# Four input and three output buffers, rows of four tokens, earlier token lists and an earlier first fetch in a causal mixing and expert kernel

## The chip, the cores and the metric

The kernel runs on one core of one Trainium2 chip. The core's engines run side by side, each through its own list of instructions in order: TensorE (PE, with its weight loads as PEld), VectorE (DVE), ScalarE (ACT), GpSimd (POOL) and SyncE (SP). An instruction that must wait for another engine or for a transfer holds everything behind it on its own engine. Transfers (DMA) are issued from SP, ACT and POOL and carried out by 16 DMA engines that all three share. The metric is device time in microseconds, the median of several runs.

## The reference, cut to what matters

```python
def _attn_ref(x, weight):                      # x (8, 3584, 192), weight (8, 7)
    w = softmax(weight, axis=-1)
    x_pad = np.concatenate([zeros((B, 6, D)), x], axis=1)
    x_unf = x_pad[:, idx, :].reshape(B, S, 7, 8, 24)      # the token and the six before it
    return einsum('hk,bskhg->bshg', w, x_unf).reshape(B, S, D)

def _moe_ref(x, w_gate, w1, w2):               # x (28672, 192); 8 experts, F = 1024
    cap = N // E                               # 3584 tokens for each expert
    logits = x @ w_gate
    order = np.argsort(-logits.flatten())      # the best pairs of token and expert first
    ...                                        # a pair is taken if its token is free and its expert has room
    for e in range(E):
        mask = assigned == e
        out[mask] = np.maximum(x[mask] @ w1[e], 0.0) @ w2[e]
```

Each of 8 heads mixes a token with the six tokens before it by 7 softmax weights. Each of the 28672 mixed tokens then goes through exactly one of 8 experts, and each expert takes exactly 3584 tokens, chosen greedily by logit.

## The kernel before

**Convolution.** The tokens are cut into 16 half batches of 1792. `load(i)` brings a half batch from DRAM to a tile `X`, 118 partitions (112 tokens and the six before them) by 16 windows by 192, in two transfers on SP: a small one for the six rows, a large one for the 112. There are three such buffers. `conv(i)` multiplies the tile, head by head, with a banded matrix `TH` on TensorE (`cv`), and ACT copies each head from PSUM to a tile `a`, of which there are two. After the eighth head ACT issues the transfer of `a` to the DRAM tensor `attn`, one row of 192 floats (768 bytes) per token, in the order of the tokens.

**Logits.** VectorE transposes `a` in 32 x 32 blocks into `aT` (`transp`, four instructions per half batch); TensorE multiplies by the gate weights (`logits`, products `pl`), ACT copies to `L`, TensorE transposes `L` (`pt`, in `logits_t`), VectorE adds a mask `pm` into the table `LT` and takes the maximum over the experts (`top`). Inside `conv(i)` the function `mid(h)`, called after each head's product, issues the transposes of half batch i - 1 with heads 0 to 3 and the logits of i - 2 with heads 2 and 5; `end(i - 2)` follows after head 7.

**Routing.** Everything from logits to lists of tokens is a row of generators: `half(0)` (threshold, placement, sorting and lists of the first eight half batches), `tail` and `tail2` (logits of half batches 14 and 15), `half(1)`, `rest`, `last`. `Steps.hook` puts their instructions between others: a planner (`Pace`) keeps an estimate of the time at which each engine will have come so far, and a step is issued when VectorE and ACT are not too far ahead of TensorE by that estimate. `tokens` turns a list's sorted entries into token numbers `ia0`, `ia`, `ib0`, `ib`.

**Feed-forward.** 56 tiles of 512 tokens. POOL fetches a tile's rows from `attn` by token number (`gather`, four indirect transfers); rows of short lists are cleared beforehand. TensorE transposes them (`px`), ACT and VectorE split them into a high and a low part (`evac`: `xa`, `xd`). `l1` makes eight blocks `ph` of hidden units, which ACT (`hh`) and VectorE (`hl`) split; `l2` makes `y` from them; `store` scatters `yo` to `out` by token number. The weights are loaded by SP into four buffers `raw`, split by ACT (high) and POOL or VectorE (low) in `wsplit`, and written to DRAM for later use; each split frees a buffer for SP's next load. The pools of the tiles (`wpool`, `wpool2`, `fh0` and others) take over the space of the convolution's buffers.

The first two tiles come from the first half of the tokens: `first(0)` and `first(1)` gather them as soon as `half(0)` has been issued. With the planner's pace that is in the last half batch; the transposes and splits of tile 0 stand behind all of the convolution.

Of the kernel before, what the change touches and what calls it, by code (L numbers as in the profile page):

```python
# [5 lines left out]
F32 = mybir.dt.float32  # L6
# [10 lines left out]
G = 256  # L17
# [95 lines left out]
def build(ctx, tc, nc, x, weight, wg, attn, LT, wk):  # L113
# [48 lines left out]
    pm = wk.tile([128, 16], F32, name="pm")  # L162

    def gate_ops():
# [9 lines left out]
        V.tensor_scalar(pi, pi, 16, None, op0=OP.bitwise_and)  # L174
        V.memset(pm, 0.0)
        for b in range(4):
            V.tensor_scalar(pm[:, 4 * b + 3:4 * b + 4], pi, -1.0 / 16, None, op0=OP.mult)
# [4 lines left out]
    def load(i):  # L182
        t = X[i] = k.xp[i % 3].tile([118, 16, D], F32, name="X")
# [10 lines left out]
    def conv(i, mid):  # L194
# [8 lines left out]
        A.dma_start(attn[i * 1792:(i + 1) * 1792].rearrange("(w p) d -> p w d", p=W), a[0:W])  # L203
# [10 lines left out]
    def transp_last(u):  # L214

        i = NHB - 1
        a = wk.tile([128, 16, 64], F32, name="X%d" % u)
        for q in range(2):
            V.transpose(a[:, 8 * q:8 * q + 8], AA[i][:, 8 * q:8 * q + 8, 64 * u:64 * u + 64])
        AT[i] = AT[i] + [a] if u else [a]  # L220

    def logits(i, u):

        if u == 0:
            AT[i].append(k.bank("pl"))
        pl = AT[i][-1]
        for c in range(4):
            w = slice(4 * c, 4 * c + 4)
            t = AT[i][u // 2].rearrange("p w (c t) -> p w c t", t=32)[:, w, u % 2] if i == NHB - 1 else AT[i][0][:, w, u]
            PE.matmul(pl[32 * c:32 * c + 32, 0:128], GF[:, u], t, start=(u == 0), stop=(u == 5))  # L230
# [13 lines left out]
    k.toeplitz, k.gate_ops, k.transp_last = toeplitz, gate_ops, transp_last  # L244
# [18 lines left out]
class Route:  # L263

# [268 lines left out]
    def tokens(self, nt, idx, e1=8, t1=None):  # L533
# [10 lines left out]
        i = v(wk.tile([128, 128], I32, name="m_j"))  # L544
        off = wk.tile([128, 1], F32, name="off")
# [16 lines left out]
    def lists(self, F, nt, h, base, idx, *part):  # L562
# [6 lines left out]
        yield from self.tokens(nt, idx, *part)  # L569
# [240 lines left out]
class General:  # L810


    def __init__(self, ctx, tc, ltab, attn, w1, w2, out, ident, drm):
# [4 lines left out]
        self.list = drm.tile([NTOK, 1], I32, name="glist")  # L818

    def consts(self):  # L820
# [20 lines left out]
        self.idi = p.tile([128, G], I32, name="g_idi")  # L841
        V.tensor_copy(self.idi, self.id)
# [131 lines left out]
    def lists(self):  # L974
# [25 lines left out]
        i1 = p.tile([128, 1], I32, name="g_i1")  # L1000
        with tc.For_i(0, G, 1) as g:
            V.tensor_copy(s1, si[:, bass.ds(g, 1)])
            V.tensor_copy(i1, self.idi[:, bass.ds(g, 1)])
# [4 lines left out]
    def ffn(self):  # L1008
# [5 lines left out]
        ix = p.tile([128, 1], I32, name="g_ix")  # L1014
# [7 lines left out]
        with tc.For_i(0, NE, 1) as e:  # L1022
# [3 lines left out]
            with tc.For_i(0, CAP // 128, 1) as t:  # L1026
                nc.sync.dma_start(ix, self.list[bass.ds(e * CAP + t * 128, 128)])
                P.indirect_dma_start(out=x, out_offset=None, in_=self.attn,
                                     in_offset=bass.IndirectOffsetOnAxis(ap=ix, axis=0),
# [15 lines left out]
                P.indirect_dma_start(out=self.out, out_offset=bass.IndirectOffsetOnAxis(ap=ix, axis=0),  # L1045
# [8 lines left out]
class FFN:  # L1054
# [19 lines left out]
    def wpool(self, ctx, j):  # L1074
        self.wpa[j] = ctx.enter_context(self.tc.tile_pool(name="wpa%d" % j, bufs=1))
# [214 lines left out]
    def run(self, idx_of, at, eng, free):  # L1290
# [4 lines left out]
        for i in range(n + 1):  # L1295
            at(i)
            if i + 2 < n:
                self.gather(i + 2, idx_of(tiles[i + 2]))
# [18 lines left out]

NL = 3


def moe_kernel(ctx, tc, x, weight, wg, w1, w2, out):
# [6 lines left out]
    with ExitStack() as cw:  # L1328
# [16 lines left out]

        order = [(e, (0,)) for e in range(NE)]
# [10 lines left out]
        def half(h):  # L1357
# [6 lines left out]
            yield from r.lists(r.F, TA, h, 0 if h else None, *((ia,) if h else (ia0, 8, 4)))  # L1364
# [190 lines left out]
```

## Time and profile before

| | us |
|---|---|
| median of three runs | 1328.89 |
| the runs | 1336.24, 1327.68, 1328.89 |
| the profiled execution's own time | 1324.88 |
| its span, first to last instruction | 1323.1 |

Busy in the span: TensorE 1251.3 us (95%), its weight loads 1077.4, VectorE 1005.2, ACT 543.2, POOL 540.1. The mean granted clock of TensorE is 0.973. The transfers moved 188.29 MB; the queue of ACT (q10, the writes of `attn`) carried 22.02 MB in 28928 pieces.

How to read the lines below. In a row of the stretches each engine's busy time in that stretch is followed by its number of instructions; then come TensorE's granted clock, the DMA engines' busy share, and GB/s. In the timeline a row has the start, the duration, the engine (a q behind it: the engine's issue of a transfer), the line of the kernel, the operation, the tile written and the tiles read, and in brackets how long the engine stood idle before and what ended that. In the chain a row is a piece of the sequence that ended last: start, length, and the work, or the transfer, it consisted of. A row of the waits names who waited, for whom, how long in total, how often, and the longest.

### The profile page before, as it was taken

The page shows a single profiled execution, that of the slowest core. Times are in us where ns is not written, and L with a number is a line of the kernel's source. Part 1 is how long each engine was busy: PE and PEld are TensorE (multiplying, and loading weights), DVE is VectorE, ACT ScalarE, POOL GpSimd, SP SyncE. Part 2 cuts the span into 40 slices and gives each one's busy share as a digit, 9 for nine tenths or more (in the row PEclk, how much of TensorE's full clock was granted, in tenths as well). Part 3 has the DMA queues.
Part 4 walks back from the last instruction along what each step waited for, and adds up shares of the span by engine and source line. Part 5 has one row for each costly group of instructions (what it writes and reads, how often), then busy time and mean ns, then how long its engine had stood idle before and what let it go on. Part 6 is the DMA issues. An engine that isn't in the chain of part 4 may idle for free.

```text
span 1323.1 us, 21760 instructions
## 1 busy us (share of the span) xinstructions
PE 1251.3 (95%) x7879; PEld 1077.4 (81%) x7879; DVE 1005.2 (76%) x2223; ACT 543.2 (41%) x1182; POOL 540.1 (41%) x547
## 2 busy tenths in 40 slices
PE   5888959999799999999999999999999999999997
PEld 2444637887789888888899999999999999999996
DVE  7369648779999988899757777777777777777772
ACT  4434434475444434443333333333333333333332
POOL 3000065586644434435224434444444444444422
PEclk9889989899899999999899999999999999999999
DMA  9999879488753433424222341432323222141100
GB/s 239 285 294 297 231 211 324 154 275 270 241 186 101 143 99 134 145 91 143 76 83 89 130 160 45 149 101 87 104 87 104 93 93 90 48 148 46 41 29 27
DMA packets 114434, 188.29 MB, mean 142 GB/s; under 512 B 12352, under 2 KB 86544, under 8 KB 110096
## 3 DMA queue, kind: packets, MB, share of 16 engines
q1 hardware_dynamic: 63888, 120.75, 28.4%
q0 software_dynamic: 21504, 44.07, 10.9%
q10 hardware_dynamic: 28928, 22.02, 5.2%
q8 instruction: 63, 1.03, 0.3%
q14 instruction: 51, 0.42, 0.1%
HBM read 114.44 MB, written 72.35 MB: 141 GB/s over the span
## 4 chain that ended last, share of the span: by engine, by line
PE 77%; DVE 9%; DMA 8%; issue 2%; POOL 2%; ACT 2%; SPq 1%; POOLq 0%; ACTq 0%; DVEq 0%
PE ph L54 34%; PE y L54 33%; DMA attn<-a 5%; PE cv L54 4%; PE bg L54 3%; DMA raw<-in_moe_w_dram 3%; DVE X L54 2%; DVE hl L54 2%; PE px L54 1%; PE pl L54 1%; DVE TH L54 1%; DVE oa L54 1%; POOL xg L1175 1%; POOL w L1156 1%; DVE r_w L54 0%
## 5 line engine op out<-in xcount | busy, mean ns | idle before, releaser
L54 PE MATMUL y<-w,hh 128*128 128x384 f32 x1792 | 543.6, 359 | 0.0
L54 ACT ACTIVATE hh<-ph 128x512 fp32r<-128x512 f32 x448 | 267.0, 596 | 492.3 <-PE ph L54 491.9
L54 PE MATMUL y<-w,hl 128*128 128x192 f32 x1792 | 451.3, 252 | 0.0
L54 DVE SCALAR_TENSOR_TENSOR hl<-ph,hh 128x512 fp32r<-128x512 f32 x448 | 308.2, 689 | 174.6 <-ACT hh L54 170.9
L54 PE MATMUL ph<-xa,w 128*128 128x512 f32 x1344 | 399.7, 406 | 2.3 <-DVE hl L54 2.3
L54 PEld LDWEIGHTS y<-w,hh 128*128 128x128 f32 x1792 | 339.4, 189 | 25.2 <-issue 7.5
L54 PEld LDWEIGHTS y<-w,hl 128*128 128x128 f32 x1792 | 344.0, 192 | 15.2
L1243 POOL DMA_INDIRECT out_dram<-yo,ib x128 | 128.0, 1000 | 294.2 <-DVE yo L54 279.4
L54 PEld LDWEIGHTS ph<-xa,w 128*128 128x128 f32 x1344 | 221.5, 191 | 22.7 <-DVE hl L54 2.9
L1243 POOL DMA_INDIRECT out_dram<-yo,ia x96 | 106.3, 1108 | 241.0 <-DVE yo L54 210.3
L54 DVE STREAM_TRANSPOSE xs<-xg 32x256 f32<-32x256 f32 (+1 forms) x512 | 188.8, 369 | 8.8
L54 PE MATMUL ph<-xd,w 128*128 128x512 f32 x448 | 179.7, 401 | 0.0
L54 PE MATMUL ph<-xd,dl 128*128 128x512 f32 x448 | 175.8, 392 | 1.2 <-DVE dl L54 1.2
L1175 POOL DMA_INDIRECT xg<-attn,ib x128 | 129.7, 1013 | 40.1 <-issue 39.8
L54 PE MATMUL cv<-X,TH 118*128 118x384 f32 x256 | 103.8, 539 | 31.1 <-ACT a L54 18.4
L1175 POOL DMA_INDIRECT xg<-attn,ia x96 | 106.8, 1112 | 28.9 <-issue 23.2
L54 ACT ACTIVATE yt<-y 128x192 f32<-128x192 f32 x224 | 73.3, 327 | 108.2 <-PE y L54 105.2
L54 DVE TENSOR_TENSOR yo<-y,yt 128x192 f32<-128x192 f32 x224 | 79.7, 356 | 42.1 <-ACT yt L54 39.3
L54 PEld LDWEIGHTS ph<-xd,dl 128*128 128x128 f32 x448 | 85.1, 190 | 21.6 <-DVE dl L54 2.6
L54 PEld LDWEIGHTS cv<-X,TH 118*128 118x128 f32 x256 | 48.0, 206 | 66.0 <-ACT a L54 26.7
L54 PEld LDWEIGHTS ph<-xd,w 128*128 128x128 f32 x448 | 85.2, 190 | 20.1 <-DVE xd L54 0.7
L54 ACT ACTIVATE a<-cv 128x384 f32<-128x384 f32 x128 | 59.2, 491 | 66.2 <-DMA attn<-a 36.8
(230 smaller groups left out, 966.6 us busy)
## 6 DMA issues: line engine op xcount, KB each, us to landing
w<-kw SPq DMA_DIRECT2D x16, 1536.0 KB
w<-kv SPq DMA_DIRECT2D x16, 1536.0 KB
X<-in_x_dram SPq DMA_DIRECT2D x16, 1344.0 KB
attn<-a ACTq DMA_DIRECT2D x16, 1344.0 KB
kw<-w SPq DMA_DIRECT2D x48, 256.0 KB
kv<-w SPq DMA_DIRECT2D x32, 384.0 KB
raw<-in_moe_w_dram SPq DMA_DIRECT2D x32, 192.0 KB
raw<-in_moe_w_dram SPq DMA_DIRECT2D x16, 256.0 KB
```

Of the source, the lines that this page charges most:

```text
L54: return f(*a, **k)
L1156: eng.tensor_tensor(lo, r[0:n], hi[0:n].bitcast(F32), op=OP.subtract)
L1175: self.nc.gpsimd.indirect_dma_start(out=t[:, b], out_offset=None, in_=self.attn[0:rows], in_offset=bass.IndirectOffsetOnAxis(ap=idx[b], ax ...
L1243: st = nc.gpsimd.indirect_dma_start(out=self.out, out_offset=bass.IndirectOffsetOnAxis(ap=idx, axis=0), in_=o, in_offset=None, bounds_chec ...
```

## The change

- `load` has four buffers X instead of three and runs three half batches ahead; `a` has three buffers instead of two.
- `attn` has another order: partition p, group g and b give row 448 g + 4 p + b of the half batch, so that a partition writes four rows, 3072 bytes, in one piece. The gathers need rows of `attn`, the scatters token numbers: `tokens` makes both (four more VectorE instructions per list), and `ja0`, `ja`, `jb0`, `jb` stand beside the old lists.
- The mask is added by ACT, as the bias of a second copy into `L`; `LT` is filled by ACT. VectorE keeps the maximum.
- Transposes and logits go through a queue `left`: one entry after each head, the transposes of half batch i - 1 in turn with the logits of i - 2. From half batch 13 on the queue rests until the first list has been issued; after that, two entries go with each head.
- `hook` sets the planner's TensorE time to at least 8.8 us per half batch plus 11, so that more routing steps are placed beside each half batch.
- When `half(0)` has been issued, `first` clears and gathers tiles 0 and 1, with POOL clearing instead of VectorE; from ten heads later on, the transposes and split of tile 0 are issued beside heads 2 and 5 of the convolution, and what is left of them behind it.
- The first weights are loaded at half batch 13 instead of 14, and split at half batches 14 and 15; the pools `fg` and `fx` have space of their own from the start.
- Half batch 15 uses the same transposes as the others, and `tail` takes the logits of 14 and 15 and the write of `LT` (`ltab`).
- The fallback `General`, which does not run with these inputs, gets lists of two columns.

```diff
-        t = X[i] = k.xp[i % 3].tile([118, 16, D], F32, name="X")
+        t = X[i] = k.xp[i % 4].tile([118, 16, D], F32, name="X")
...
-        A.dma_start(attn[i * 1792:(i + 1) * 1792].rearrange("(w p) d -> p w d", p=W), a[0:W])
+        A.dma_start(attn[i * 1792:(i + 1) * 1792].rearrange("(g p b) d -> p g (b d)", g=4, b=4),
+                    a[0:W].rearrange("p (g b) d -> p g (b d)", b=4))
...
-            A.activation(L, pl[:, 0:128], AF.Copy)
+            l, m = (t.rearrange("p (w t) -> p w t", t=32) for t in (L, pl[:, 0:128]))
+            A.activation(l[:, :, 0:16], m[:, :, 0:16], AF.Copy)
+            A.activation(l[:, :, 16:32], m[:, :, 16:32], AF.Identity, bias=pm)
...
-        V.tensor_tensor(o, v, pm.rearrange("p (b q) -> p b q", q=4)[:, None].to_broadcast([128, 8, 4, 4]), op=OP.add)
+        A.activation(o, v, AF.Copy)
...
+        V.scalar_tensor_tensor(y, i, -127.0 / 4, x, op0=OP.mult, op1=OP.add)
...
+        V.scalar_tensor_tensor(y, gi, 28.0, y, op0=OP.mult, op1=OP.add)
...
+        V.scalar_tensor_tensor(y, i, 4.0, y, op0=OP.mult, op1=OP.add)
+        V.tensor_scalar(row, y, 4.0, None, op0=OP.mult)
...
+PERIOD, START = 8.8, 11.0
+LAG = 13
...
-        k.ap = pool(ca, "ap", 2, **right)
-        k.xp = [None] * 3
+        k.ap = pool(ca, "ap", 3, **right)
+        k.xp = [None] * 4
...
-        def first(e):
-            ff.gather(e, [ia0[:, e, b:b + 1] for b in range(4)], NTOK // 2, V)
...
-        def hook():
+        def first():
+            for e in range(2):
+                ff.gather(e, [ja0[:, e, b:b + 1] for b in range(4)], NTOK // 2, P)
+
+        todo = [partial(f, 0, *a) for u in range(2) for f, a in ((lambda i, u: ff.transp(i, u, r.bg()), (u,)), (ff.evac, (u,)))]
+        got, left = [], []
...
+        def hook(at):
+            nc.pe = max(nc.pe, PERIOD * at / 8 + START)
             bg.hook(1.5)
-            if len(bg.gens) == 5:
-                gather()
+            if not got and len(bg.gens) == 4:
+                first()
+                got.append(at)
+            elif got and at >= got[0] + 10 and at % 8 in (2, 5) and todo:
+                for _ in range(2):
+                    todo.pop(0)()
...
             def mid(h):
-                if i and h < 4:
-                    k.transp(i - 1, h)
-                if 2 <= i and h in (2, 5):
-                    for u in range(3):
-                        k.logits(i - 2, h // 4 * 3 + u)
-                if i == 15 and h in (4, 5):
+                if i and h == 0:
+                    for u in range(4):
+                        left.append(partial(k.transp, i - 1, u))
+                        if i > 1:
+                            left.append(partial(gate, i - 2, u) if u < 3 else partial(end, i - 2))
+                for _ in range(2 if got else 1):
+                    if left and (i < LAG or got):
+                        left.pop(0)()
+                if i >= 14 and h % 2:
                     ff.wsplit(-1, P)
...
-                hook()
+                hook(8 * i + h)
```

What this makes of the engines' lists shows at three places. TensorE in an early half batch, before (`cv` is one head's convolution, `pl` the logits' products, `pt` the transpose of `L`):

```order
L54 MATMUL cv<-X,TH 128x384 x3
L54 MATMUL pl<-aT,c_mu 32x128 x12
L54 MATMUL cv<-X,TH 128x384 x3
L54 MATMUL pl<-aT,c_mu 32x128 x12
L54 MATMUL cv<-X,TH 128x384 x2
L54 MATMUL pt<-ident,L 128x128
```

The same stretch of TensorE now:

```order
L55 MATMUL cv<-X,TH 128x384 x2
L55 MATMUL pl<-aT,c_mu 32x128 x8
L55 MATMUL cv<-X,TH 128x384 x2
L55 MATMUL pl<-aT,c_mu 32x128 x8
L55 MATMUL cv<-X,TH 128x384 x2
L55 MATMUL pl<-aT,c_mu 32x128 x8
L55 MATMUL cv<-X,TH 128x384 x2
L55 MATMUL pt<-ident,L 128x128
```

The logits come in three groups of eight products between pairs of heads. TensorE at the end of the convolution, before (`px` and `bg<-ident,xg` are the transposes of a fetched tile, `ph` the first feed-forward products):

```order
L54 MATMUL cv<-X,TH 128x384 x3
L54 MATMUL pl<-aT,c_mu 32x128 x12
L54 MATMUL cv<-X,TH 128x384 x2
L54 MATMUL px<-ident,xg 128x128 x4
L54 MATMUL bg<-ident,xg 64x128 x4
L54 MATMUL pt<-ident,L 128x128
L54 MATMUL ph<-xa,w_1629 128x512 x3
```

TensorE at the same place now:

```order
L55 MATMUL cv<-X,TH 128x384
L55 MATMUL pt<-ident,L 128x128
L55 MATMUL bg<-ident,xg 128x128 x4
L55 MATMUL cv<-X,TH 128x384 x2
L55 MATMUL bg<-ident,xg 64x128 x4
L55 MATMUL ph<-xa,w_1522 128x512 x3
```

The first four transposes of tile 0 stand ahead of the last two heads. POOL from the clear of the first `dl` on, before (`w` and `dl` are low parts of weights, the DMA rows are gathers):

```order
L1078 MEMSET dl 64x1024
L1156 TENSOR_TENSOR w_1629<-raw,w_1629 128x512
L1156 TENSOR_TENSOR dl<-raw,w_1629 64x512
L1175 DMA xg<-attn,ia_105 128x192 x8
L1156 TENSOR_TENSOR w_1629<-raw,w_1629 128x512
L1156 TENSOR_TENSOR dl<-raw,w_1629 64x512
L1078 MEMSET dl 64x1024
L1175 DMA xg<-attn,ia_105 128x192 x4
L1156 TENSOR_TENSOR w_1790<-raw,w_1790 128x2x192 x4
```

POOL from there on now:

```order
L1082 MEMSET dl 64x1024
L1160 TENSOR_TENSOR w_1522<-raw,w_1522 128x512
L1177 MEMSET xg 128x768
L1179 DMA xg<-attn,ja_109 128x192 x4
L1177 MEMSET xg 128x768
L1179 DMA xg<-attn,ja_109 128x192 x4
L1160 TENSOR_TENSOR dl<-raw,w_1522 64x512
L1160 TENSOR_TENSOR w_1522<-raw,w_1522 128x512
L1160 TENSOR_TENSOR dl<-raw,w_1522 64x512
L1082 MEMSET dl 64x1024
L1179 DMA xg<-attn,ja_109 128x192 x4
L1160 TENSOR_TENSOR w_1808<-raw,w_1808 128x2x192 x4
```

The two clears have come in, and the gathers stand ahead of three of the first four splits instead of two.

More of the change, by code (lines that the diff above doesn't have):

```diff
@@ L1 @@
 from contextlib import ExitStack
+from functools import partial
 import concourse.bass as bass
@@ L161, in build @@
     GF = wk.tile([128, 6, 32], F32, name="c_mu")
[L162 removed]
+    pm = wk.tile([128, 1], F32, name="pm")
     def gate_ops():
@@ L568, in lists @@
         yield from self.gather(nt, base is None)
-        yield from self.tokens(nt, idx, *part)
+        yield from self.tokens(nt, idx, row, *part)
     def counts(self, n0):
@@ L1369, in rest @@
             yield from r.final(NL)
-            yield from r.lists(r.F, TB, 1, None, ib0, NL, 4)
+            yield from r.lists(r.F, TB, 1, None, ib0, jb0, NL, 4)
         def last():
-            yield from r.lists(r.F, TB, 0, 1, ib)
+            yield from r.lists(r.F, TB, 0, 1, ib, jb)
         def tail():
-            for u in range(6):
-                k.logits(14, u)
-                if u % 2:
-                    yield PEA if u == 5 else None
-            end(14)
+            for i in (14, 15):
+                for u in range(3):
+                    gate(i, u)
+                    yield PEA if u == 2 else None
+                end(i)
+            nc.sync.dma_start(r.ltab, LT)
+            c1.close()
             cs.close()
@@ L1385, in tail @@
             yield
-        def tail2():
-            for u in range(6):
-                k.logits(15, u)
-                if u % 2:
-                    yield PEA if u == 5 else None
-            end(15)
-            nc.sync.dma_start(r.ltab, LT)
-            yield
-        bg = Steps(nc, r, (half(0), tail(), tail2(), half(1), rest(), last()))
-        bg.keep = 5
+        bg = Steps(nc, r, (half(0), tail(), half(1), rest(), last()))
+        bg.keep = 4
         cs, c1, ca, cl, cc = (ExitStack() for _ in range(5))
-        cx = [ExitStack() for _ in range(3)]
+        cx = [ExitStack() for _ in range(4)]
+        ff.xg = pool(cw, "fg", 2)
+        ff.xs = pool(cw, "fx", 2)
         k = build(cs, tc, nc, x, weight, wg, attn, LT, wk)
@@ L1472, in moe_kernel @@
         nc.lat, nc.las = (0.8, 1.2)
-        gather()
+        if not got:
+            first()
         bg.keep = 0
-        ff.xs = pool(cw, "fx", 2, **late)
-        for u in range(2):
-            ff.transp(0, u, r.bg() if u else None)
-            ff.evac(0, u)
-        for _ in range(2):
-            ff.wsplit(-1, P)
-        for u in (1, 2):
-            k.transp_last(u)
-        end(13)
-        for c in (ca, c1, cl):
+        for f in left + todo:
+            f()
+        for u in range(4):
+            k.transp(15, u)
@@ L1485, in moe_kernel @@
+        for c in (ca, cl):
             c.close()
         k.bank = lambda name: r.bg()
-        k.lrow = lambda: oh.tile([128, 128], F32, name="oa")
         ff.py = pool(cw, "py", 2, space=PSUM, **late)
@@ L1490, in moe_kernel, with idx_of @@
         ff.op = pool(cw, "fo", 3, **late)
+        ff.xp = pool(cw, "fp", 1, **late)
         ff.hp = [pool(cw, "fh0", 1, **late), None]
         ff.wpool(cw, 1)
-        def idx_of(tile_):
+        def idx_of(tile_, rows=False):
             e, t = tile_[1]
             if t == 0:
-                return [ia0[:, e, b:b + 1] for b in range(4)]
+                return [(ja0 if rows else ia0)[:, e, b:b + 1] for b in range(4)]
             if t < 3:
@@ L1500, in idx_of @@
                     bg.drain(2)
-                return [ia[:, e, 4 * t + b:4 * t + b + 1] for b in range(4)]
+                return [(ja if rows else ia)[:, e, 4 * t + b:4 * t + b + 1] for b in range(4)]
             if t == 3 and e < NL:
```

96 lines of the change are left out of this document (44 added, 52 removed).

## The prediction

> **What bounds the kernel now.** I read the busy table by slices first, then three stretches, the chain of waits up to 260 us, the list of waits, and last the timeline at the places these named.
>
> ```profile
> core 0: us, PE busy (x) PEld busy (x) DVE busy (x) ACT busy (x) POOL busy (x), PEclk, DMA share, GB/s
> 20.00:169.50 149.50, 129.32 (x1111) 74.55 (x1109) 98.15 (x213) 63.03 (x145) 7.63 (x25) 0.92 0.95 277
> 169.50:205.00 35.50, 20.56 (x164) 14.51 (x164) 13.37 (x24) 12.03 (x25) 22.68 (x22) 0.81 0.76 232
> 205.00:1323.10 1118.10, 1093.39 (x6593) 984.23 (x6591) 878.30 (x1932) 458.28 (x991) 502.38 (x477) 0.98 0.36 120
> ```
>
> Three stages: convolution to 169.5 us, a handover to 205, the feed-forward tiles after. TensorE is busy 1093.4 of the last 1118.1 us; the change leaves those tiles alone, so what it does must come from the first two rows. There TensorE is idle 20.2 and 14.9 us, and its granted clock is lower, 0.92 and 0.81.
>
> ```profile
> by line: DMA attn<-a 23.1%; PE cv L54 19.0%; PE bg L54 6.3%; PE y L54 5.6%; PE pl L54 5.3%; DVE TH L54 4.9%; PE ph L54 4.5%; issue 4.0%; DVE oa L54 3.6%; DMA raw<-in_moe_w_dram 3.6%; POOL xg L1175 2.7%; ACT a L54 2.1%; DMA kd<-dl 1.7%; POOL
> ...
> 49.50 13.41 DMA attn<-a
> ...
> 76.78 14.74 DMA attn<-a
> ...
> 99.47 10.77 DMA attn<-a
> ```
> ```profile
> ACT a L54 <- DMA attn<-a: 36.8, 8, 9.3
> ```
>
> The chain to 260 us spends its largest share, 23%, in the write of a half batch to DRAM. A write takes 11 to 15 us to land, a half batch's work about 7.5, and there are two buffers `a`: ACT waits for the write of two half batches ago, 36.8 us in eight waits, and TensorE behind ACT.
>
> ```profile
> DMA packets 1209, 0.92 MB, mean 229 GB/s; under 512 B 14, under 2 KB 1209, under 8 KB 1209
> ```
> ```profile
> DMA packets 2200, 1.68 MB, mean 373 GB/s; under 512 B 17, under 2 KB 2200, under 8 KB 2200
> ```
> ```profile
> DMA packets 1077, 0.83 MB, mean 344 GB/s; under 512 B 1, under 2 KB 1077, under 8 KB 1077
> ```
>
> These are the DMA view for 77.5 to 81.5 us (loads of x alone: 229 GB/s), 85 to 89.5 (loads and write together: 373) and 110 to 112.4 (a write alone: 344). The DMA engines show 95% busy over the whole stage, yet moved 277 GB/s: by rate they have a quarter in hand.
>
> **The change, part by part.**
>
> *Third buffer `a`, fourth buffer X.* With three buffers ACT waits for the write of three half batches ago, issued two paces (15 us or more) earlier: longer than the 14.7 us of the slowest quoted. The 36.8 us go; what is late next is the work itself. Its pace is read where nothing waited:
>
> ```profile
> 25.91 1.75 ACTq L203 DMA_DIRECT2D attn<-a  x1
> ...
> 76.78 0.31 ACTq L203 DMA_DIRECT2D attn<-a  x1
> 84.31 0.31 ACTq L203 DMA_DIRECT2D attn<-a  x1
> 99.47 0.31 ACTq L203 DMA_DIRECT2D attn<-a  x1
> 106.79 0.31 ACTq L203 DMA_DIRECT2D attn<-a  x1
> 115.28 0.31 ACTq L203 DMA_DIRECT2D attn<-a  x1
> ```
> ```profile
> 20.00:169.50 149.50, 13.03 (x185) 0.92 0.95 277
> ```
>
> From 76.78 to 84.31 is 7.53 us, from 99.47 to 106.79 is 7.32: 7.43 for a half batch. Half batch 1 ends at 25.91, where no buffer was short, and stays there. Fourteen follow: 104.0 us. The list work on TensorE (tile bg, 13.0 us) lies beside nothing on that engine and comes on top; so do the first tile's transposes, which now stand in the last half batch (1.75 us, row below). 25.9 + 104.0 + 13.0 + 1.75 = 144.7.
>
> ```profile
> L54 DVE STREAM_TRANSPOSE aT<-a 128x768 f32<-128x768 f32 x60 | 54.1, 949 | 1.5 <-ACT a L54 1.5
> L54 DVE TENSOR_TENSOR oa<-irep,q 128x1024 bf16<-128x1024 bf16 x16 | 10.0, 681 | 0.0
> L54 DVE TENSOR_TENSOR LT<-pt,pm 128x128 f32<-128x128 f32 x13 | 3.7, 288 | 36.2 <-PE pt L54 36.2
> ```
>
> VectorE is the next in line. A half batch's four transposes cost 3.8 us; in the two to three half batches that hold the 16 `oa` builds (0.68 each), it has about 3.8 + 0.4 + 6 = 10.2 us, where TensorE has 7.43 + 3.5 = 10.9. They are nearly level, and TensorE's list products wait for VectorE in order; I add 3 us. The 0.288 us LT addition moves from VectorE to ACT (which also gets one more activation per half batch): ACT is busy 63 of 149.5 us, so this costs nothing unless ACT becomes late. The wider spread of logits (8 products after each head instead of 12 twice) keeps their count. **The convolution then ends at about 148 us, 21.5 before 169.5.**
>
> *Rows of 3072 bytes instead of 768.* Bytes stay, pieces fall to a quarter. Between no gain (both at 373 GB/s: 2.75 MB in 7.4 us per half batch) and a loss if the longer pieces crowd out the loads (9.1, below). The new pace, (148 − 25.9)/14 = 8.7, asks 316 GB/s. I take no cost: 373 was reached with both queues busy.
>
> *Lists ahead, first tile fetched beside the convolution.*
>
> ```profile
> 167.02 0.19 DVE L54 SCALAR_TENSOR_TENSOR ia<-m_j,m_x 128x32 int32<-128x32 int32 x1
> ...
> 170.06 0.31 ACTq L203 DMA_DIRECT2D attn<-a  x1
> ...
> 170.39 1.25 POOL L1175 DMA_INDIRECT xg<-attn,ia  x1 [0.17 <-issue]
> ...
> 179.50 1.75 PE L54 MATMUL px<-ident,xg 128*128 128x128 f32 x4 [9.99 <-DMA xg<-attn,ia]
> ...
> 186.16 0.95 POOL L1078 MEMSET dl<- 64x1024 f32 x1 [0.30 <-PE px L54]
> ...
> 192.26 3.88 POOL L1156 TENSOR_TENSOR w<-raw,w 128x384 fp32r<-128x384 f32 x4
> ...
> 193.67 0.79 SPq L1111 DMA_DIRECT2D raw<-in_moe_w_dram  x1
> ...
> 203.22 0.63 ACT L54 ACTIVATE w<-raw 128x512 fp32r<-128x512 f32 x1 [0.58 <-DMA raw<-in_moe_w_dram]
> ...
> 204.69 0.34 PE L54 MATMUL y<-w,hh 128*128 128x384 f32 x1
> ```
>
> Before, the list is ready at 167.0, TensorE stands 10 us until the gathered rows land, and the first `y` comes at 204.7, 35.2 after the convolution's end. That `y` hangs on POOL: after eight gathers (1.3 us each) and its share of splitting weights, it clears the second `dl` at 186.16, gathers tile 2, splits four pieces from 192.26; each frees a buffer for SP's next load, and ACT waits for that load in front of `hh`. From 186.16 to 204.69 is 18.5 us, and none of it is changed.
>
> What moves is when POOL gets there. In the change the list is made in half batch 13; the four gathers of tile 0 need some 9.2 us from issue (170.39) to the transposes (179.50), and POOL's first split and clear stand 2 us ahead of them. They are issued from head 1 of half batch 14 on, and wanted after head 5 of half batch 15: twelve heads, 12.6 us at 1.05 a head. Hidden, with 1 to 2 us to spare; without that cover TensorE stands in the middle of half batch 15 behind the transposes, and the remaining heads with it. POOL is also passed by two clears of xg (before 0.70 on VectorE each, about 0.75 here by the 0.95 of `dl`) and three of four weight splits now come behind the eight gathers: done about 1 to 2 us after the end of the convolution. Then the clear of the second `dl` lies in the space of the buffers `a`, and must wait for the last write:
>
> ```profile
> q10 hardware_dynamic: 1808, 1.38, 71.6%
> ```
>
> That is the DMA view from 161.7 to 168.1: a write issued at 161.70 with no load beside it moved its whole 1.38 MB in 6.4 us. Issue 0.55 after the end, 6.4 to move, some 0.3 to be seen: POOL goes on 7.2 us after the end, instead of 16.7 (186.16 − 169.5). **This saves 9.4 us.**
>
> *The rest.* Four more VectorE instructions per list, some 0.2 us each (`ia` row): 0.8 on the first list, inside that spare time; the later lists lie under the tiles, where VectorE is busy 878 of 1118 us. The last logits stay inside tile 0, as before. Weight loads, stores, and SP's order are the same but for the 1 MB `ltab` write, a few places earlier. One wait stays on SP, by the shared completion semaphores:
>
> ```profile
> 83.79 0.27 SPq L188 DMA_DIRECT2D X<-in_x_dram  x1
> 91.54 0.31 SPq L192 DMA_DIRECT2D X<-in_x_dram  x1
> ```
>
> The large part of a load was issued 7.75 us behind its small part, just as the write of 76.78 landed (76.78 + 14.74 = 91.52). In the change the small part has this wait, for the write of as long ago, but the load is for one half batch further ahead; with four buffers it may come a pace late without harm.
>
> *Sum.* 21.5 + 9.4 = 30.9; 1 back for POOL's and VectorE's additions. The profiled execution's own time is 1324.88 (span 1323.1 and 1.8 around it): 1324.9 − 29.9 = 1295. The median of the runs is 1328.89, 0.3% above the profile; I give **1296**.
>
> **The Trainium skill at one place.** The 1276 pieces of the write and 924 of the load in the 373 GB/s window show both queues served about evenly with pieces of equal size. "DMA: Bandwidth & Descriptors" of the Trainium skill (Queues, rings and completion order) states that each DMA engine takes turns between the queues packet by packet; by it, a queue with longer packets gets more of the engine, which speaks against this change and is the first rival. No run here yet shows unequal pieces.
>
> **Rivals.**
> 1. *The long pieces crowd out the loads.* If the queues take turns by piece, the write gets 4/5 of 373 GB/s while it lasts: 1.38 MB in 4.6 us, the load 0.34 MB; its other 1.03 MB run alone at 229, 4.5 us. The pace is 9.1, set by DMA. Half batch 2's load is there by 24 to 25 us; the 13 later ones by 143, and half batch 15 follows, 8 to 9 us: end at 152. Time 1299 to 1300. For it: loads alone never were near 373. Against: it needs loads alone for half the time, and four buffers allow several in flight.
> 2. *The fetch is late or the handover keeps its length.* The gathers wait behind loads and writes; TensorE stands up to 10 us in half batch 15, or the 35.2 us stay. 148 + 35.2 instead of 148 + 25.7: 1305.
> 3. *Loads and writes in turn, slower.* If each write holds back the next load (by its pieces, or by SP's wait), they never overlap: 1.38 MB at 229 and at 344 are 6.0 + 4.0, and two landings of about 1.5 us: 13 us a half batch. End at 25 + 13 × 13 + 8 = 202: 1348. It is slower than before from a pace of 11.3 on. Against: the 373 GB/s window shows them side by side.
> 4. *No change.* The pace stays where it was (143.6 us for 14, 10.3 each) since VectorE, not the writes, held it: then only 9 us or less are left, 1316. Against: VectorE is busy 98 of 149.5 us.
>
> **How the numbers follow.** Chances: my forecast 0.62, with 1287 to 1301 from an end of the convolution at 142 (no extra for VectorE, 2 less of clock loss) to 154; rival 1 0.16; rival 2 0.13; rival 3 0.04; rival 4 0.05. The range takes the forecast and rivals 1 and 2: 1285 to 1309. About 1% is what a measurement of this kernel can tell from no change: below 1315.6 lie the forecast and rivals 1 and 2, 0.91; rival 4 counts as same, 0.05; rival 3 as slower, 0.04.
>
> **What would show it.** Waits of ACT `a` for DMA attn under 8 us in total; attn issues 7.4 apart up to the lists and about 10 to 11 in the three half batches with `oa`; the last `cv` near 148; xg's transposes in the last half batch with under 3 us of wait (more: rival 2); the clear of the second `dl` about 7 us behind the last `cv` and the first `y` 26 behind it; the tiles unchanged at 1118 us. A DMA rate of 300 GB/s with `cv` waiting for X is rival 1. The forecast is wrong if `cv` waits for X for more than 10 us, or if the first `y` comes later than 180.

## The result, and the profile after

| | before | after |
|---|---|---|
| median of six runs, us | 1330.18 | 1321.69 |
| the runs, us | 1327.68 to 1336.24 | 1319.91 to 1325.35 |
| span of the profiled execution, us | 1323.1 | 1318.1 |

The ratio of after to before is 0.995, 95% interval 0.9927 to 0.9973: half a per cent faster, where 1296 (0.975) was forecast, with 1309 as the upper end. The stretches of the changed kernel, with the columns as before (the convolution, the handover to the first `y`, the tiles):

```profile
core 0: us, PE busy (x) PEld busy (x) DVE busy (x) ACT busy (x) POOL busy (x), PEclk, DMA share, GB/s
20.00:165.60 145.60, 129.92 (x1118) 71.69 (x1117) 95.61 (x200) 71.28 (x175) 20.73 (x38) 0.96 1.02 297
165.60:190.30 24.70, 18.35 (x157) 12.86 (x155) 11.07 (x17) 9.85 (x24) 10.17 (x10) 0.93 0.69 226
190.30:1318.10 1127.80, 1097.71 (x6594) 987.75 (x6592) 879.42 (x1944) 456.57 (x994) 506.77 (x477) 0.98 0.37 120
```

The convolution ends at 165.6 instead of 169.5 (148 was forecast), the handover takes 24.7 us instead of 35.2 (25.7 was forecast), and the tiles take 1127.8 instead of 1118.4 (unchanged was forecast). -3.9 - 10.5 + 9.4 make the 5.0 us by which the spans differ.

The chain of waits up to 260 us, by line, had 23.1% in the write `attn<-a` before; now it has 3.3% there, and 12.3% in the loads:

```profile
by line: PE cv L55 17.2%; DMA X<-in_x_dram 12.3%; PE bg L55 8.5%; issue 7.7%; PE y L55 7.0%; PE ph L55 6.7%; PE pl L55 5.7%; DVE aT L55 3.4%; DVE X L55 3.4%; SPq L187 3.3%; DMA attn<-a 3.3%; SPq L167 3.0%; SPq L190 2.6%; DMA raw<-in_moe_w_d
```

Two readings say where the convolution's time stands. First the waits of TensorE in it, then TensorE's timeline at the two longest of them, then ACT's issues of the writes:

```profile
PE cv L55 <- DMA X<-in_x_dram: 9.4, 3, 4.7
PE bg L55 <- DVE m_x L55: 3.0, 4, 1.0
```
```profile
39.01 2.90 PE L55 MATMUL cv<-X,TH 118*128 118x384 f32 x4 [4.67 <-DMA X<-in_x_dram]
...
62.02 1.56 PE L55 MATMUL cv<-X,TH 118*128 118x384 f32 x4
...
67.12 2.90 PE L55 MATMUL cv<-X,TH 118*128 118x384 f32 x4 [3.42 <-DMA X<-in_x_dram]
```
```profile
25.79 0.31 ACTq L202 DMA_DIRECT2D attn<-a  x1
35.07 0.31 ACTq L202 DMA_DIRECT2D attn<-a  x1
49.11 0.32 ACTq L202 DMA_DIRECT2D attn<-a  x1
56.83 0.31 ACTq L202 DMA_DIRECT2D attn<-a  x1
64.42 0.31 ACTq L202 DMA_DIRECT2D attn<-a  x1
78.48 0.31 ACTq L202 DMA_DIRECT2D attn<-a  x1
```

ACT no longer waits for a write; TensorE waits for loads. After each long wait the same four products take 2.90 us instead of 1.56: TensorE's clock is halved for a while (0.5 in the trace's clock records). The Trainium skill, "TensorE: Matmul & The Clock Gate" (What's actually happening), says that an idle window of about 3.4 us drops the clock to half until a busy one has passed; the trace agrees behind the first of these two waits, with a half-clock record of 3.4 us; behind the second it lasts 6.8. Half batches 4 and 5 run 7.72 and 7.59 us apart, as forecast; the two with a wait, 3 and 6, take 14.0 and 14.1. The five from 25.79 to 78.48 take 52.7 us, where 5 x 7.43 = 37.2 was forecast: 15.5 lost. The waits for loads are 9.4 of these; the 10.2 us at half clock cost up to half their length, 5.1 more (an estimate). The nine from there to the last issue at 166.18 take 87.7, where 9 x 7.43 + 13 + 1.75 + 3 = 84.6 was forecast.

What the DMA engines did meanwhile is seen in two windows of their view, 27.2 to 34.2 us (writes 0 and 1 and the load of half batch 3) and 46 to 54 us (loads alone). Behind each queue are packets, MB and its share of 16 engines; q10 has the writes, q1 the loads:

```profile
DMA packets 1279, 2.84 MB, mean 406 GB/s; under 512 B 36, under 2 KB 465, under 8 KB 1278
## 3 DMA queue, kind: packets, MB, share of 16 engines
q10 hardware_dynamic: 838, 2.50, 88.8%
q1 hardware_dynamic: 440, 0.33, 14.1%
```
```profile
DMA packets 1906, 1.45 MB, mean 181 GB/s; under 512 B 24, under 2 KB 1906, under 8 KB 1906
```

The writes moved nearly two pieces for each piece of the load, and a write's piece is four times as long: they took 2.50 of 2.84 MB. While writes run, the load stands nearly still; when it is alone it makes 181 GB/s. (From 27 to 35.5 us the counts are 904 and 863, because the load catches up in pieces as the writes end.) One more thing changed: SP's issues of the small parts of the loads last 1.9 to 8.7 us from half batch 4 on, where they took 0.3 us before. From 46.8 to 49 us, around the end of one of them (39.71 to 47.56), the DMA engines were only 59.5% busy with the load and moved 128 GB/s. No run takes these long issues apart from the length of the pieces; with 768-byte pieces they last up to 5.3 us. By the trace's records of single pieces the loads follow one another without a gap (each begins within 0.1 us of the end of the one before), from half batch 2 at 15.66 to half batch 15 at 134.05: 118.4 / 13 = 9.1 us each on average (6.1 to 12.5).

The handover did what it was to do: no wait of TensorE for xg, and POOL's clear of the second `dl`:

```profile
163.73 0.60 PE L55 MATMUL bg<-ident,xg 128*128 128x128 f32 x4
```
```profile
174.88 0.95 POOL L1082 MEMSET dl<- 64x1024 f32 x1 [9.69 <-DMA attn<-a]
```

The clear comes 9.3 us behind the convolution, the first `y` (190.27) 15.4 behind that.

### The profile page after: what moved, and what is told of

The parts are those of the page before. It is cut to its first block, busy times and chain, and to the rows that moved or that the text cites. A ratio compares the mean times of both kernels' runs of the same rounds, so it can differ in the third digit from the quotient of the medians.

```text
span 1318.1 us, 21815 instructions
## 1 busy us (share of the span) xinstructions
PE 1253.2 (95%) x7879; PEld 1076.2 (82%) x7879; DVE 1001.2 (76%) x2215; ACT 547.7 (42%) x1214; POOL 544.8 (41%) x549
## 4 chain that ended last, share of the span: by engine, by line
PE 79%; DVE 9%; DMA 4%; issue 3%; SPq 2%; POOL 1%; ACT 1%; POOLq 0%; DVEq 0%; ACTq 0%
PE ph L55 35%; PE y L55 35%; PE bg L55 4%; PE cv L55 3%; DVE X L55 3%; DMA X<-in_x_dram 2%; DVE hl L55 2%; DMA raw<-in_moe_w_dram 1%; PE pl L55 1%; PE px L55 1%; DVE aT L55 1%; SPq L187 1%; DMA attn<-a 1%; SPq L167 1%; SPq L190 1%
## 5 line engine op out<-in xcount | busy, mean ns | idle before, releaser
L55 PEld LDWEIGHTS y<-w,hl 128*128 128x128 f32 x1792 | 345.6, 193 | 15.4
L55 PEld LDWEIGHTS ph<-xa,w 128*128 128x128 f32 x1344 | 221.5, 191 | 30.3 <-DVE hl L55 10.7
L1179 POOL DMA_INDIRECT xg<-attn,jb x128 | 130.0, 1016 | 40.1 <-issue 39.8
L1179 POOL DMA_INDIRECT xg<-attn,ja x96 | 107.8, 1123 | 28.9 <-issue 25.2
```

The lines of the kernel that those rows point to most:

```text
L55: return f(*a, **k)
L1179: self.nc.gpsimd.indirect_dma_start(out=t[:, b], out_offset=None, in_=self.attn[0:rows], in_offset=bass.IndirectOffsetOnAxis(ap=idx[b], ax ...
```

## The experiments

For each kernel the table has the ratio of its time to that of the kernel before on the same chip (95% interval), the time for half batches 2 to 6 and 7 to 15 (from the issues of the writes), the end of the convolution, how far behind it the first `y` comes, and how far behind it the ninth tile's first `y`, all from the timelines, in us.

| kernel | ratio | 2 to 6 | 7 to 15 | end | first y | ninth tile |
|---|---|---|---|---|---|---|
| before | 1 | 50.9 | 93.3 | 169.5 | +35.2 | +227.2 |
| after | 0.995 (0.9927 to 0.9973) | 52.7 | 87.7 | 165.6 | +24.7 | +225.3 |
| changed_again | 0.9945 (0.9923 to 0.9967) | 51.9 | 89.7 | 166.8 | +24.9 | +224.4 |
| pieces768 | 0.9885 (0.9854 to 0.9916) | 41.6 | 89.4 | 154.9 | +26.8 | +225.4 |
| pieces1536 | 0.9893 (0.9867 to 0.9919) | 45.3 | 95.8 | 166.3 | +23.3 | +222.6 |
| two_a | 0.994 (0.992 to 0.9961) | 49.2 | 92.4 | 165.5 | +26.9 | +224.1 |
| pieces768_two_a | 1.0001 (0.9975 to 1.0028) | 49.7 | 92.4 | 167.3 | +26.1 | +225.9 |
| before_a3 | 0.9889 (0.9859 to 0.9918) | 40.2 | 85.9 | 151.3 | +33.7 | +229.3 |
| no_loads | | 45.3 | 89.6 | 159.8 | | |
| load_act | 0.9915 (0.9888 to 0.9943) | 46.2 | 86.9 | 161.8 | +27.6 | +227.0 |
| p768_norow_act | 1.0078 (1.0053 to 1.0104) | 48.7 | 96.3 | 180.8 | +26.8 | +224.6 |
| late_fetch | 0.9926 (0.9901 to 0.9951) | 49.3 | 91.9 | 163.2 | +29.6 | +224.3 |
| p768_norow | 0.9881 (0.9852 to 0.991) | 41.8 | 92.1 | 154.5 | +27.8 | +224.5 |
| p768_norow_vp0 | 0.9894 (0.9867 to 0.9921) | 41.5 | 93.0 | 155.3 | +28.7 | +227.4 |
| p768_late | 0.9879 (0.9843 to 0.9916) | 42.0 | 89.0 | 153.2 | +32.7 | +227.5 |
| dve_plus | 0.9932 (0.99 to 0.9965) | 41.9 | 92.1 | 154.6 | +28.2 | +231.2 |
| pool_plus | 0.9889 (0.9846 to 0.9932) | 41.9 | 93.1 | 155.3 | +30.0 | +225.8 |
| pe_plus | 0.997 (0.995 to 0.999) | 44.8 | 91.8 | 158.3 | +28.9 | +234.6 |

### The length of the pieces

**pieces768**: the changed kernel, writing in 768-byte pieces as before; the gathers take token numbers again.

```diff
-        A.dma_start(attn[...].rearrange("(g p b) d -> p g (b d)", g=4, b=4), a[0:W].rearrange("p (g b) d -> p g (b d)", b=4))
+        A.dma_start(attn[i * 1792:(i + 1) * 1792].rearrange("(w p) d -> p w d", p=W), a[0:W])
...
-                self.gather(i + 2, idx_of(tiles[i + 2], True))
+                self.gather(i + 2, idx_of(tiles[i + 2]))
...
-                ff.gather(e, [ja0[:, e, b:b + 1] for b in range(4)], NTOK // 2, P)
+                ff.gather(e, [ia0[:, e, b:b + 1] for b in range(4)], NTOK // 2, P)
```

> Writes of the convolution in 768-byte pieces again, gathers by token number as before; buffers, lists and fetch stay as in the changed kernel. Theory A (the 3072-byte pieces take the DMA engines from the loads): load and write share evenly, a pair (1.34 MB each) takes 7.4 to 8 us instead of the 9.1 us start to start measured in the changed kernel, half batch 15 is in at 127 to 133 us instead of 145.1, the convolution ends at 153 to 158 instead of 165.6 and the time is 1309 to 1314. Theory B (the two queues together deliver about 300 GB/s over a pair, whatever the pieces): half batch 15 in at 145, convolution end 164 to 168, time 1318 to 1324. Theory C (TensorE and VectorE hold the second half anyway): loads early, but the convolution still ends at 162 to 166 and the time is 1317 to 1322.

Half batch 15 was in at 130.4 us (145.1 with long pieces) and the convolution ended at 154.9: theory A in both places. The time, 1305.70, lies below A's 1309 to 1314, beside 1323.48 for the kernel before on the same chip. The ratio's interval lies wholly below that of the changed kernel. The DMA view of this kernel from 39.8 to 61.6 us:

```profile
DMA packets 10576, 8.05 MB, mean 369 GB/s; under 512 B 109, under 2 KB 10575, under 8 KB 10575
## 3 DMA queue, kind: packets, MB, share of 16 engines
q10 hardware_dynamic: 5274, 4.01, 54.8%
q1 hardware_dynamic: 5301, 4.02, 54.4%
```

Equal pieces, equal bytes, and 369 GB/s for 22 us on end. TensorE's wait for X is down to 2.4 us:

```profile
PE cv L55 <- DMA X<-in_x_dram: 2.4, 4, 0.8
```

**pieces1536**: the write in pieces of two rows. The gathers keep the row numbers of the changed kernel, so they fetch other tokens' rows.

```diff
-        A.dma_start(attn[...].rearrange("(g p b) d -> p g (b d)", g=4, b=4), ...)
+        A.dma_start(attn[...].rearrange("(g p b) d -> p g (b d)", g=8, b=2), ...)
```

> Writes of the convolution in 1536-byte pieces (2 rows each), half of the changed kernel's. The gathers still compute places for 3072-byte pieces, so they fetch other tokens' rows; their number and sizes are the same. Theory A (queues take turns by piece): between the two measured ends: the load gets a third of the engines beside a write, half batch 15 in at 135 to 141 us (130.4 with 768, 145.1 with 3072), convolution end 158 to 162. If only the row order or the address pattern of the 3072-byte layout counted and not the length of the pieces: half batch 15 in at 143 to 147, or at 129 to 132.

The load's progress lies between the ends: half batches 2 to 6 took 45.3 us (41.6 and 52.7), half batch 15 was in at 139.3. The convolution ended at 166.3 instead of 158 to 162, but the profiled execution (span 1316.0) lies above the median of this kernel (1313.08); its half batches 7 to 15 were slow, 95.8: near their end TensorE waits 3.7 us for ACT's copy `L` and then runs at half clock for 6.8 us from 155.4 on. What made that copy late was not looked into. In the loads the length of the pieces counts, step by step.

### The buffers

**two_a**: the changed kernel with two buffers `a`.

```diff
-        k.ap = pool(ca, "ap", 3, **right)
+        k.ap = pool(ca, "ap", 2, **right)
```

> The changed kernel with two buffers a instead of three. If the write's landing is what the third buffer took off the path: ACT waits for DMA attn 20 to 40 us again, the convolution ends at 175 to 185 and the time is 1331 to 1341. If the loads hold the pace whatever the writes do (A or B): the waits come back but lie beside the wait for X, the convolution ends at 166 to 170, time 1320 to 1326.

ACT waits for writes again:

```profile
ACT a L55 <- DMA attn<-a: 18.5, 5, 6.5
```

Yet the second reading held in the main, the convolution ends at 165.5 (166 to 170 was expected, and 1320 to 1326 for the time, which is 1314.89): the waits took the place of waits for loads. TensorE waits 5.9 us for ACT's copies and 4.5 for loads, where it waited 9.4 for loads with three buffers. (The ratio, 0.994, is that of the changed kernel.)

**pieces768_two_a**: both edits together.

> 768-byte pieces and two buffers a instead of three. If the third buffer is worth nothing once loads come early: convolution end 154 to 158, time within 3 us of the same with three buffers (1306 where before is 1323.5). If it carries the gain: ACT waits for DMA attn 20 us or more, convolution end 162 to 168, time 1313 to 1319.

Here the third buffer is everything: 1.0001 with two, 0.9885 with three. ACT's waits:

```profile
ACT a L55 <- DMA attn<-a: 22.6, 6, 9.7
```

So with short pieces the third buffer is worth 1.2%, with long ones nothing; and without the third buffer the long pieces gain 0.6%.

**before_a3**: the kernel before, with one edit.

```diff
-        k.ap = pool(ca, "ap", 2, **right)
+        k.ap = pool(ca, "ap", 3, **right)
```

> The kernel before with one edit: three buffers a instead of two (three X, 768-byte pieces, late lists and fetch as before). If the third buffer is the part of the change that is worth something, and the 3072-byte pieces ate it: ACT's waits for DMA attn fall from 36.8 us below 12, the convolution ends at 156 to 162 instead of 169.5 and the time is 7 to 13 us below before (ratio 0.990 to 0.995). If three X are too few to let the loads run on: cv waits for X, convolution end 165 to 169, ratio 0.997 to 1.000.

That line alone gives 0.9889, the end of the convolution at 151.3 is earlier than the 156 to 162 expected. No wait of ACT for a write above 0.5 us is left, and the convolution's stretch moves 315 GB/s:

```profile
20.00:151.30 131.30, 122.85 (x1111) 72.25 (x1109) 98.14 (x213) 65.84 (x144) 7.85 (x26) 0.97 0.99 315
```

Three buffers X and 768-byte pieces were enough. Set beside pieces768, which keeps all other parts of the change and comes to 0.9885, it shows that these parts together bring nothing that the ratio can tell: the first `y` follows the convolution 6.9 us sooner there, and the convolution ends 3.6 later.

### The loads

**no_loads**: the convolution runs on the first four half batches.

```diff
     def load(i):
-        t = X[i] = k.xp[i % 4].tile([118, 16, D], F32, name="X")
+        if i > 3:
+            X[i] = X4[i % 4]
+            return
+        t = X[i] = X4[i] = k.xp[i % 4].tile([118, 16, D], F32, name="X")
...
```

> Loads of half batches 4 to 15 are left out (the convolution reads the four it has over and over), everything else stays. If my sum for TensorE and VectorE was right and only the loads failed it (theories A and B): no wait for X, attn issues 7.4 to 7.7 us apart up to the lists, the convolution ends at 146 to 152 us. If TensorE and VectorE hold the pace (theory C): the convolution ends at 160 us or later although nothing waits for X.

Its routing then meets other logits and ends in the fallback, so only the convolution is read. Its end, 159.8, lies just below the 160 of the second reading. Half batches 4 and 5 came 7.59 us apart each; half batch 3 still waited for its load, which the first two writes held up (13.5 us instead of 7.6, so 6 us of the 45.3); without these the end would be near 154 (an estimate), between the readings. The last nine took 89.6 with no load of x at all, 5 us above my sum: there it is not the loads that hold.

**load_act**: half of each load's windows through ACT's queue.

```diff
-        nc.sync.dma_start(t[6:118], ...)
+        nc.sync.dma_start(t[6:118, 0:8], ...)
+        nc.scalar.dma_start(t[6:118, 8:16], ...)
```

> Half of every load (rows 8 to 15 of each partition) goes to ACT's DMA queue, behind the write of the half batch before; the other half stays on SP's. If a lone queue is what limits a load by itself to 215 to 224 GB/s: with two queues loads reach 300 GB/s or more when no write runs, the first load is in at 6 us instead of 8.7, half batch 15 at 125 to 135 and the convolution ends at 152 to 158. If the limit lies in the rows' places or the engines, the rate stays at 220 and the convolution ends at 164 to 170; later than that if half a load standing behind a write costs more than it brings.

Two queues did not make loads alone faster. From 3 to 8.5 us, where only loads run, this kernel and then the changed one:

```profile
DMA packets 1528, 1.10 MB, mean 201 GB/s; under 512 B 111, under 2 KB 1528, under 8 KB 1528
```
```profile
DMA packets 1816, 1.36 MB, mean 248 GB/s; under 512 B 51, under 2 KB 1816, under 8 KB 1816
```

Part of this gap is the start, in which the two queues had little to do yet: from 5.2 to 8.5 us the rates are 245 and 258 GB/s. The expected end was missed too: 161.8 is better than 164 to 170, and half batches 2 to 6 took 46.2 us. The likely reason, not tested, is that half of each load now stands in the queue that gets the larger share.

**p768_norow_act**: the same on top of 768-byte pieces, without the row lists.

> 768-byte pieces, no row lists, and half of every load on ACT's DMA queue. If the loads still hold half batches 2 to 6 (8.3 us apart with 768-byte pieces against 7.6 without loads): 7.6 to 7.8 there, convolution end 149 to 152 instead of 154.9, ratio 2 to 4 thousandths lower. If the engines' total holds them, or half a load stands too long behind a write: 154 to 158, no lower ratio.

Worse than foreseen, 180.8. From 23.5 us on each of ACT's issues of half a load lasts 2.9 to 6.2 us here (0.3 to 0.9 in load_act), and ACT's copies stand behind it: TensorE waits 20.2 us for them. Why the issues take so long is open.

### The handover and the tiles

**changed_again**: no edit.

> The changed kernel itself, on the same chip as the three others. It serves as their base, and asks whether the tiles' 1127.8 us (first y to the end; 1118.4 before) come from the code: then 1126 to 1130 again. If they come from where TensorE's stalls and the half-clock stretches behind them happened to fall: 1118 to 1124, and the time 3 to 8 us lower against before than at the first measurement. The convolution ends at 164 to 167 either way.

The tiles took 1127.0 us again (191.7 to 1318.7): it is not the accident of one execution.

**late_fetch**: the first tile's gathers, transposes and splits behind the convolution.

```diff
-LAG = 13
+LAG = 16
...
-            if not got and len(bg.gens) == 4:
+            if False:
```

> The changed kernel with the first tile's gathers and transposes behind the convolution, as before the change (and the transposes and logits of the convolution not held back for them). If the handover's gain was the fetch and POOL's earlier clear of dl: convolution end 162 to 166, first y 33 to 37 us behind it instead of 24.7, time 8 to 11 us above the changed kernel. If the gathers hide behind the last write anyway: first y 25 to 28 behind it, time within 3 us of the changed kernel.

The first `y` came 29.6 behind the convolution, between the readings, and the time was not higher but lower (1317.3 against 1320.75, the intervals overlap). The ninth tile began at the same distance, 224.3.

**p768_norow**: 768-byte pieces, and no row lists.

```diff
-        V.scalar_tensor_tensor(y, i, -127.0 / 4, x, op0=OP.mult, op1=OP.add)
...
-        V.scalar_tensor_tensor(y, gi, 28.0, y, op0=OP.mult, op1=OP.add)
...
-        V.scalar_tensor_tensor(y, i, 4.0, y, op0=OP.mult, op1=OP.add)
-        V.tensor_scalar(row, y, 4.0, None, op0=OP.mult)
```

> The changed kernel with 768-byte pieces, and without the four VectorE instructions per list that compute the row places (not needed then). If these instructions take back what the shorter handover gave: from the end of the convolution to the start of the ninth tile's second matrix 218 to 222 us instead of the 222.6 to 227.2 of all kernels so far, ratio to before 0.984 to 0.987. If something else holds that stretch: 224 to 227 again, ratio 0.987 to 0.990 (0.9885 with the instructions).

No difference: the four instructions are free, as forecast.

**p768_norow_vp0**: on top of that, the pieces of the splits that went to VectorE.

```diff
-        VP = (1, 3)
+        VP = ()
```

> The same, and while lists are made all eight pieces of a weight's split go to GpSimd; two of the eight went to VectorE. If VectorE holds the stretch from the end of the convolution to the ninth tile (busy 94.6 of 100 us from 285 to 385): it shrinks by 4 to 10 us. If GpSimd or the weights hold it: it grows by 3 us or more.

2.9 us longer, but VectorE's busy time in the stretch did not fall (181.8 after 178.0), so this says nothing on VectorE.

**p768_late**: p768_norow with the edit of late_fetch.

> 768-byte pieces, no row lists, and the first tile's gathers and transposes behind the convolution again. If the stretch from the end of the convolution to the ninth tile is 224 to 227 us whatever the first y does: the convolution ends 2 to 4 us earlier (151 to 153 against 154.5), first y 28 to 31 behind it, ratio to before 0.985 to 0.988. If the earlier first y is worth its time: ratio 0.990 to 0.994.

The first `y` at +32.7, 5 us later, costs 3 us up to the ninth tile, the convolution ends 1.3 earlier, and the ratio is the same.

**dve_plus, pool_plus, pe_plus**: p768_norow with more work for one engine at the second list: each `oa` built twice on VectorE, 64 clears of 0.205 us on GpSimd, the products of the list done twice on TensorE (in `sort`, where `base == 0` marks that list).

```diff
+                for _ in range(2 if base == 0 else 1):
                     V.tensor_tensor(a, self.irep[:, :, 0:per], ...)
```
```diff
+                if base == 0:
+                    s = self.wk.tile([128, 128], F32, name="m_y")
+                    for _ in range(4):
+                        nc.gpsimd.memset(s, 0.0)
```
```diff
+                    for _ in range(2 if base == 0 else 1):
                         PE.matmul(ps[:, c:c + 16], a[:, :, u], ...)
```

> On the kernel with 768-byte pieces and no row lists: VectorE builds each of the 16 oa of the second list (tiles 1 and 2) twice, 16 x 0.68 = 11 us more on VectorE. If VectorE holds the stretch from the end of the convolution to the ninth tile (224.5 us there): it grows by 8 to 15 us. If it has slack: by under 4.

> The same base with 64 clears of a 128x128 tile on GpSimd at the same places (about 0.2 us each, 10 to 14 us more on GpSimd). If GpSimd (its splits of weights, gathers and stores, in order) holds the stretch: 8 us or more on top of 224.5. If it has slack: under 4.

> The same base with the 128 small products of the second list done twice on TensorE (about 10 us more by the spans of 16 products in 1.3 us). If TensorE's own work fills the stretch: 7 to 11 us on top of 224.5. If it waits for others at these places: under 4, since the products go where it stood.

The stretch from the end of the convolution to the ninth tile, in p768_norow, dve_plus, pool_plus and pe_plus:

```profile
154.50:379.00 224.50, 199.23 (x1260) 173.78 (x1259) 177.99 (x363) 110.31 (x261) 130.49 (x115) 0.92 0.72 236
```
```profile
154.60:385.80 231.20, 200.54 (x1256) 172.14 (x1255) 195.28 (x358) 110.70 (x261) 125.41 (x114) 0.93 0.71 229
```
```profile
155.30:381.10 225.80, 198.17 (x1261) 171.47 (x1260) 180.63 (x363) 110.93 (x261) 143.41 (x179) 0.93 0.71 235
```
```profile
158.30:392.90 234.60, 209.02 (x1387) 183.00 (x1386) 177.73 (x363) 110.21 (x261) 130.43 (x115) 0.91 0.69 226
```

9.8 us more on TensorE make it 10.1 longer, 17.3 more on VectorE 6.7, 12.9 more on GpSimd 1.3. TensorE's own work fills the stretch, VectorE is close behind it (6.7 lies between its two readings), GpSimd has room.

## Why the prediction was wrong, step by step

**Third buffer `a`: right, in mechanism and nearly in size.** ACT's waits for writes are gone; with this edit alone the convolution ends at 151.3, where 148 was forecast. The fourth X was not needed for it.

**"Rows of 3072 bytes ... I take no cost: 373 was reached with both queues busy": the step that failed.** 373 GB/s had been reached with pieces of equal size, and in that window the load had 924 of the 2200 pieces and bytes in the same proportion. Beside pieces of four times the length it moved 0.33 of 2.84 MB. Of the 18.5 us by which the last write was issued too late (166.18; the sum had 147.65), 15.5 lie in half batches 2 to 6. Undoing this one edit gives 11.1 of these back (52.7 to 41.6) and 10.7 us of the convolution; the other 4.4 stay with short pieces, and no run says what takes them. This step alone does not account for the miss: with it undone the ratio is 0.9885, which for the 1328.89 of the prediction is 1314, still above 1309. The rest lies in a second step, the tiles below.

**Rival 1 was this case, and it was given 0.16.** Its pace of 9.1 is what the loads did, to the tenth; that it agrees so closely is luck, since its terms did not: beside the load the writes had 88% of the bytes and not 4/5, at 406 GB/s and not 373, and loads alone made 181 to 258 GB/s instead of 229. Its sign came too: TensorE waits for X while the stretch moves 297 GB/s, although the wait, 9.4 us, stays just under the 10 that were to refute the forecast. The row that decides stood in the prediction, loads alone at 229 GB/s, and "several in flight" was no argument against it: in one queue they run one after the other. The rule of the Trainium skill named there ("DMA: Bandwidth & Descriptors", section Queues, rings and completion order: the engines take turns between queues, packet by packet) agrees with the equal counts of pieces768 over 22 us, 5274 and 5301. One piece for one piece, as the rival had it, is not what the trace shows for unequal ones: 838 to 440 from 27.2 to 34.2 us. Yet the rival's own end, 152, was too early, because it let TensorE follow 8 to 9 us behind the last load. The last load was in at 145.1, but TensorE had lost 15 us in the first half, and in the second half it had the lists to do, so nothing could be caught up: a stage bound by loads first and by TensorE later costs the sum of both, not the larger.

**Work with the lists: somewhat too small.** The last nine half batches take 87.7 us instead of 84.6, and 85.9 to 89.6 in before_a3, pieces768 and no_loads.

**Handover: right in size, and worth little.** 24.7 us instead of the forecast 25.7, with the clear 2.1 later and the way from there 3.1 shorter: two errors that nearly cancel, so the size is right partly by luck. The second step that failed is "the tiles unchanged at 1118 us": they took 1127.8. Up to the ninth tile only 1.9 us of the 10.5 were left, and in all the kernels without added work that start lies 222.6 to 229.3 us behind the convolution, with the first `y` anywhere from 23.3 to 35.2. The waits of TensorE in the first tiles, before (204.7 to 355.6) and after (190.3 to 349.8):

```profile
PE bg L54 <- DVE r_cc L54: 6.9, 2, 5.6
PE ph L54 <- DVE hl L54: 2.0, 1, 2.0
PE bg L54 <- DVE oa L54: 1.9, 4, 0.8
PE px L54 <- DVE xa L54: 1.2, 2, 0.7
PE ph L54 <- DVE dl L54: 1.2, 3, 0.5
```
```profile
PE bg L55 <- DVE r_cc L55: 6.6, 2, 5.6
PE ph L55 <- DVE hl L55: 5.2, 2, 2.6
PE bg L55 <- DVE oa L55: 2.2, 2, 1.7
PE ph L55 <- DVE dl L55: 2.2, 4, 1.5
```

And the first four tiles as a whole, before and after:

```profile
204.70:305.60 100.90, 95.41 (x646) 83.61 (x645) 79.15 (x153) 58.70 (x140) 62.62 (x55) 0.95 0.75 252
```
```profile
190.30:299.70 109.40, 99.30 (x646) 86.61 (x645) 82.86 (x157) 59.12 (x143) 65.74 (x55) 0.92 0.72 238
```

The same 646 products take 8.5 us longer: TensorE stands 4.6 us more (10.1 instead of 5.5), nearly all for VectorE (waits of 5.5 us before and 9.6 after in these four tiles), and is busy 3.9 more at a lower clock. By the trace's clock records TensorE ran at half speed for 13.7 us of the handover and 9.3 us of these tiles before, for 3.4 and 18.5 after. VectorE has 3.7 us more to do in them. So the idle time of the handover had been cover: for VectorE's list work, and for half-clock time that met little work there. That these two are what took the gain is read from the profiles and from the three runs with added work; no run removed them. For the same reason the hidden fetch, which worked, has no price that these runs can show (late_fetch, p768_late).

**The rest held**: row lists, the mask on ACT, and, as far as the runs tell, SP's waits. Rival 4 (1316) comes nearest to the time, but not by its cause: the convolution's pace did change when the pieces and the buffers did, and there TensorE waits for loads and writes, not for VectorE.

## What to carry to other kernels

A rate at which two queues shared the DMA engines holds only for the sizes of pieces that were measured: lengthening the pieces of one queue takes the engines from the other, and if the other is the one that is waited for, better descriptors make the stage slower. Judge a bundle of edits by runs of its parts: here one buffer alone gave twice the gain of the whole. And before a start is moved earlier, look at what else the idle time was covering: add work to one engine at a time behind it and see which one moves the end.

## What the runs showed of the hardware

- Two busy queues with pieces of equal size moved 5274 and 5301 of them in 22 us. With pieces of 3072 bytes beside 768 the counts were 838 to 440 while the writes ran, and 88% of the bytes went to the long ones.
- Long pieces raise the engines' total (406 GB/s in that window against 369) and still slow the stage.
- Loads of x alone ran at 181 to 258 GB/s over one queue and at 245 over two: a second queue is no remedy. What limits them stays open.
- An issue of a load can hold its engine: 0.3 us in the kernel before, up to 8.7 us on SP in the changed kernel, 2.9 to 6.2 us on ACT in p768_norow_act, where TensorE paid for it.
